# Eight PSUM banks in one pool: retention and feed-forward share them, masks and outputs work on one bank of both units

One NeuronCore of a Trainium2 chip. The metric is device time of the core in microseconds, lower is better; the time before is 290.71 us.

## The reference

Retention (attention without softmax, with a decay mask) feeds a squared-relu feed-forward. Cut to what matters:

```python
batch, n_heads, seq, head_dim = (8, 8, 576, 64)          # q, k, v, float32
gamma = 1.0 - 2.0 ** (-5.0 - np.arange(H))
Dmat = np.where(rel >= 0, gamma[:, None, None] ** rel[None], 0.0)
x = ((q @ k.T / 8) * Dmat) @ v                            # per batch and head
x = x.transpose(0, 2, 1, 3).reshape(4608, 512)
g = np.maximum(x @ w_in, 0.0) ** 2                        # 512 -> 2048
out = g @ w_out                                           # 2048 -> 512, float32
```

## The kernel before

The work is cut into 36 units of 128 tokens, two to a group, 18 groups. For each group TensorE (PE) does

- retention in 64x64 matmuls: scores `psc`, state sums `psS`, outputs `psO`. VectorE (DVE) masks the scores into `rT`, and multiplies the outputs by the decays into `xT`, the input of the feed-forward;
- feed-forward, first half: eight banks `ph` (two row blocks each), relu on ScalarE (ACT) into `rl`, the square on ACT or DVE into `gT`;
- feed-forward, second half, from the third group on as seven Strassen products `po` of eight matmuls, some on sums `gS` that DVE makes. The products live in three banks of the group, called a, b and c.

A Python list scheduler fixes each engine's order at build time. It knows banks only as counters.

```python
    ps_ff = ctx.enter_context(tc.tile_pool(name="ps_ff", bufs=4, space=bass.MemoryType.PSUM))
    ps_ret = ctx.enter_context(tc.tile_pool(name="ps_ret", bufs=1, space=bass.MemoryType.PSUM))
    sched = Schedule(dict(ff=4, prS=1, prO=1, g=3, ...))      # counters: four banks, a score pair, an output pair
    # ... cut ...
    def after_scores(g, t, key):
        for s, u in enumerate(units_of(g)):                   # one instruction a unit, half of both banks
            def fm(s=s, u=u):
                r = tile_of["rT", u] = work.tile([P, 2, NP, 64], FP16, name="rT", tag="rT")
                tile_of["masking", g] = nc.vector.tensor_tensor(
                    out=r, in0=tile_of["psc", g][:, :, cols(s)].rearrange("p a (n i) -> p a n i", i=64),
                    in1=mask.rearrange("p (o r i) -> p o r i", o=1, r=1).to_broadcast([P, 2, NP, 64]), op=ALU.mult)
            m = add("DVE", key + s, 0.7, fm, deps=[t] + ..., acq=("rT",))
        sched.free("prS", [m])
    # ... cut: add_ret, a group not joined with the next ...
            def fa():
                emit_scores(g)
                emit_sums(g, "prO")
            t = add("PE", base + 3, ..., fa, ..., acq=("prS", "prO") if nf else ("prS",))
            after_scores(g, t, base + 5)
    # ... cut: a Strassen product takes its bank from the feed-forward's four ...
                        tile_of["pb", g, bank] = ps_ff.tile([P, HM], FP32, name="po", tag="ff")
```

## Time and profile before

| | before |
|---|---|
| time, median of 3 | 290.71 us (290.68 to 290.76) |
| span of the profiled run, granted clock | 289.1 us, 1.00 |
| busy share PE, DVE, ACT | 98%, 63%, 65% |
| first ph starts / last matmul ends | 17.7 us / 284.8 us |

PE sets the time, and busy share alone does not say how tightly. So the measure used throughout is start to start: from the first matmul of one stretch of feed-forward or of one retention block to the first of the next one, in the timeline.

### The profile page before, as it was taken

What the parts mean: (1) busy time and instruction counts of PE and PEld (TensorE: products, weight loads), DVE (VectorE), ACT (ScalarE), POOL (GpSimd) and SP (SyncE); (2) the same over time, 40 slices, a digit from 0 to 9 for tenths busy, and PEclk for the clock granted to TensorE, in tenths of its full rate; (3) what the DMA queues carried; (4) which work ended last, traced back from release to release, by engine and by line L of the source; (5) the groups of instructions that cost most, each with busy time, mean ns of one, the idle gap of its engine ahead of it and who ended that gap; (6) DMA issues with size and microseconds to landing.
All of it is one profiled execution on the core that took longest, in us unless ns stands there. A gap on an engine that the chain in (4) does not pass through costs nothing.

```text
span 289.1 us, 9988 instructions
## 1 busy us (share of the span) xinstructions
PE 282.1 (98%) x4322; PEld 234.3 (81%) x4322; DVE 182.4 (63%) x381; ACT 188.2 (65%) x361; POOL 84.1 (29%) x121
## 2 busy tenths in 40 slices
PE   8999999999999999999999999999999999999994
PEld 3568755788888888888888888888888888888883
DVE  3772368769585657736686857575777775455622
ACT  5459964685757676767756767676767676747830
POOL 5660035443333243342506061505250500000000
PEclk9999999999999999999999999999999999999999
DMA  7999999999999689999788799899995920201004
GB/s 202 274 208 206 249 291 267 219 203 202 221 188 198 153 201 199 217 219 219 154 199 168 172 194 205 163 196 206 225 182 151 181 76 2 75 2 73 2 8 139
DMA packets 139436, 49.94 MB, mean 173 GB/s; under 512 B 118144, under 2 KB 135040, under 8 KB 139392
## 3 DMA queue, kind: packets, MB, share of 16 engines
q1 hardware_dynamic: 134848, 44.84, 75.3%
q0 software_dynamic: 4224, 4.19, 8.8%
q8 instruction: 34, 0.56, 0.8%
q10 hardware_dynamic: 320, 0.26, 0.4%
q14 instruction: 10, 0.08, 0.1%
HBM read 36.70 MB, written 9.44 MB: 160 GB/s over the span
## 4 chain that ended last, share of the span: by engine, by line
PE 91%; DMA 3%; issue 2%; POOL 2%; DVE 0%; POOLq 0%; DVEq 0%
PE ph L859 44%; PE po L951 34%; PE po L899 5%; PE psO L345 4%; DMA w_in<-in_moe_w_in_dram 3%; PE psc L345 2%; PE psS L345 2%; PE psT L423 1%; POOL mask L215 0%; POOL vx L404 0%; POOL w_in L319 0%; DVE o L974 0%; POOL mask L207 0%; DVE p L1003 0%; POOL mask L211 0%
## 5 line engine op out<-in xcount | busy, mean ns | idle before, releaser
L859 PE MATMUL ph<-xT,w_in 128*128 128x256 f16 x1152 | 139.9, 273 | 0.1
L859 PEld LDWEIGHTS <-w_in 128*128 128x128 f16 x1152 | 110.9, 98 | 14.8 <-DMA w_in<-in_moe_w_in_dram 0.3
L867 ACT ACTIVATE rl<-ph 128x512 f16<-128x512 f32 x144 | 84.5, 588 | 52.5 <-PE ph L859 50.9
L877 ACT ACTIVATE gT<-rl 128x512 f16<-128x512 f16 x118 | 74.4, 631 | 3.4
L951 PEld LDWEIGHTS <-gS 128*128 128x128 f16 x512 | 49.8, 98 | 5.9
L951 PE MATMUL po<-wT,gS 128*128 128x256 f16 x384 | 52.1, 273 | 0.0
L928 DVE TENSOR_TENSOR gS<-gT,gS 128x512 f16<-128x512 f16 x64 | 32.8, 517 | 14.2 <-ACT gT L877 13.5
L951 PEld LDWEIGHTS <-gT 128*128 128x128 f16 x384 | 37.1, 98 | 4.5
L928 DVE TENSOR_TENSOR gS<-gT 128x512 f16<-128x512 f16 x64 | 30.9, 485 | 12.6 <-ACT gT L877 12.5
L359 POOL CAST kq<-k 128x512 f16<-128x512 f32 x28 | 18.6, 663 | 61.4 <-DMA k<-in_k_dram 60.2
L951 PE MATMUL po<-w_out,gT 128*128 128x256 f16 x256 | 34.7, 273 | 0.0
L371 POOL TENSOR_TENSOR v<-v,vdec_full 128x512 f16<-128x512 f32 x24 | 25.4, 1057 | 21.9 <-DMA v<-in_v_dram 20.9
L359 POOL CAST kq<-q 128x512 f16<-128x512 f32 x28 | 18.5, 660 | 30.8 <-DMA q<-in_q_dram 30.6
L964 ACT COPY u<-po 128x256 f32<-128x256 f32 x32 | 11.8, 369 | 19.1 <-PE po L951 18.9
L974 DVE TENSOR_TENSOR o<-po,u 128x256 f32<-128x256 f32 x31 | 13.0, 420 | 16.3 <-PE po L951 10.0
L736 DVE TENSOR_TENSOR xT<-psO,gam_full 128x512 f16<-128x512 f32 x28 | 18.1, 684 | 6.3 <-PE psO L345 6.2
L682 DVE TENSOR_TENSOR rT<-psc,mask 128x512 f16<-128x512 f32 x28 | 18.3, 683 | 4.6 <-PE psc L345 4.5
L879 DVE TENSOR_TENSOR gT<-rl 128x512 f16<-128x512 f16 x26 | 12.8, 492 | 12.6 <-ACT rl L867 11.9
L974 DVE TENSOR_TENSOR o<-po,p 128x256 f32<-128x256 f32 x17 | 7.2, 423 | 17.8 <-ACT u L964 8.8
L951 PE MATMUL po<-wT,gT 128*128 128x256 f16 x128 | 16.8, 273 | 0.0
L951 PE MATMUL po<-w_out,gS 128*128 128x256 f16 x128 | 16.8, 273 | 0.0
L899 PE MATMUL po<-w_out,gT 128*128 128x512 f16 x64 | 15.7, 380 | 0.0
(78 smaller groups left out, 224.0 us busy)
## 6 DMA issues: line engine op xcount, KB each, us to landing
out_dram<-o SPq DMA_DIRECT2D x32, 256.0 KB, 3.7
k<-in_k_dram SPq DMA_DIRECT2D x24, 256.0 KB, 4.8
q<-in_q_dram SPq DMA_DIRECT2D x24, 256.0 KB, 5.1
v<-in_v_dram SPq DMA_DIRECT2D x24, 256.0 KB, 4.9
pair<-in_k_dram SPq DMA_DIRECT2D x4, 512.0 KB, 7.0
pair<-in_q_dram SPq DMA_DIRECT2D x4, 512.0 KB, 7.2
pair<-in_v_dram SPq DMA_DIRECT2D x4, 512.0 KB, 7.0
w_in<-in_moe_w_in_dram POOLq DMA_DIRECT2D x4, 512.0 KB, 8.9
```

What stands on the lines that cost most here:

```text
L345: t = nc.tensor.matmul(out_, lhsT=lhsT, rhs=rhs, start=start, stop=True, skip_group_check=True, tile_position=(64 * row, 64 * col))
L359: op(out=out_.rearrange("p (n b a d) -> p n b a d", n=2, b=2, a=2), in_=in_.rearrange("p (n a b) d -> p n b a d", n=2, a=2))
L371: nc.gpsimd.tensor_tensor(out=t, in0=tile_of["v32", u], in1=vdec[kind].rearrange("p (h o) -> p h o", o=1).to_broadcast([P, H, D]), op=ALU. ...
L682: tile_of["masking", g] = nc.vector.tensor_tensor(out=r, in0=tile_of["psc", g][:, :, cols(s)].rearrange("p a (n i) -> p a n i", i=64), in1 ...
L736: nc.vector.tensor_tensor(out=tile_of["x", g][:, :, s * P:(s + 1) * P].rearrange("p n (c i) -> p c n i", c=2), in0=tile_of["psO", g][:, :, ...
L859: nc.tensor.matmul(tile_of["ph", g, fb][:, j, :], lhsT=w_in16[:, m, fi * P:(fi + 1) * P], rhs=tile_of["x", g][:, m, :], start=(m == 0), st ...
L867: nc.scalar.activation(out=t, in_=tile_of["ph", g, fb], func=ACTF.Relu)
L877: nc.scalar.activation(out=t, in_=rl, func=ACTF.Square)
L899: nc.tensor.matmul(tile_of["po", u], lhsT=tile_of["g", g][:, fi, s * P:(s + 1) * P], rhs=w_out16[:, fi, :], start=(fi == 0), stop=(fi == N ...
L928: nc.vector.tensor_tensor(out=Sx(k, h), in0=in0(h), in1=in1(h), op=op)
L951: nc.tensor.matmul(tile_of["pb", g, bank], lhsT=left(i), rhs=right[:, i, :], start=(start and i == 0), stop=(i == HF - 1), skip_group_chec ...
L974: nc.vector.tensor_tensor(out=o_tile(u)[:, half * HM:(half + 1) * HM], in0=bank(x), in1=tile_of[name, g], op=ALU.add)
```

## The change

The intent: no bank sits idle in a fixed pair; a bank of scores comes free after one mask, not two; feed-forward may use up to eight. The diff, cut to its core:

```diff
-    ps_ff = ctx.enter_context(tc.tile_pool(name="ps_ff", bufs=4, space=bass.MemoryType.PSUM))
-    ps_ret = ctx.enter_context(tc.tile_pool(name="ps_ret", bufs=1, space=bass.MemoryType.PSUM))
+    ps_ff = ctx.enter_context(tc.tile_pool(name="ps_ff", bufs=8, space=bass.MemoryType.PSUM))
-    sched = Schedule(dict(ff=4, prS=1, prO=1, ...
+    sched = Schedule(dict(ff=8, prS=1, prO=1, ...
+    def banks(name):
+        return [ps_ff.tile([P, 512], FP32, name=name, tag="ff") for i in range(2)]
     # after_scores: one instruction a bank, both units
-        for s, u in enumerate(units_of(g)):
-            def fm(s=s, u=u):
+        for a in range(2):
+            def fm(a=a):
-                    out=r, in0=tile_of["psc", g][:, :, cols(s)].rearrange("p a (n i) -> p a n i", i=64),
+                    out=tile_of["rT", g][:, :, a],
+                    in0=tile_of["psc", g][a].rearrange("p (s n i) -> p s n i", s=2, i=64),
+            sched.free("ff", [m])
     # after_outs: likewise xT, one instruction a bank
-                    in0=tile_of["psO", g][:, :, cols(at)].rearrange("p c (n i) -> p c n i", i=64),
+                    in0=tile_of["psO", g][c].rearrange("p (s n i) -> p s n i", s=n, i=64),
     # retention blocks take banks from the common counter
-                    acq=("prS", "prO") if nf else ("prS",))
+                    acq=("prS", "ff", "ff") + (("prO", "ff", "ff") if nf else ()))
-                     acq=("prO", "prS"))
+                     acq=("prO", "prS", "ff", "ff", "ff", "ff"))
     # the first sum quad waits for the mask by an explicit dependency, where reuse of the pair imposed it
+                first_waits.append(tile_of["masking", g + 1])
     # ... cut: the same in the other retention blocks; an unused option (SHARED) removed ...
```

More of the change, by code (lines that the diff above doesn't have):

```diff
@@ L234 @@
     PAIRED = 8
-    SHARED = ()
     FIRST = ["k0", "q0", "v0", "k2", "q2", "v2", "w0", "w1", "w2", "w3", "w4", "w5", "w6", "w7", "k4", "q4", "v4", "k6", "q6", "v6"]
-    sched = Schedule(dict(ff=4, prS=1, prO=1, g=3, ld=5, wst=4, kq=7, v16=7, rT=4, x=3, rl=3, o=4, p1=2, u2=2, u4=2,
+    sched = Schedule(dict(ff=8, prS=1, prO=1, g=3, ld=5, wst=4, kq=7, v16=7, rT=2, x=3, rl=3, o=4, p1=2, u2=2, u4=2,
                           R=5, Rm=2, kqT=6))
@@ L463, in fs @@
             def fs(e=e, tag=tag):
-                ps = rT["ps", e] = ps_ret.tile([P, 2, 512], FP32, name="psc", tag=tag)
+                ps = rT["ps", e] = banks("psc")
                 rT[e] = cast.tile([P, 2, NP, P], FP16, name="rx", tag="kq16")
@@ L467, in fs @@
                     for a, s in ((0, 0), (1, 1), (0, 1), (1, 0)):
-                        quad(ps[half(s), a, hp * P:(hp + 1) * P], kqT(s)[half(a), hp, half(e)], kqT(s)[half(a), NP + hp, :],
+                        quad(ps[a][half(s), hp * P:(hp + 1) * P], kqT(s)[half(a), hp, half(e)], kqT(s)[half(a), NP + hp, :],
                              a, s)
-            t = add("PE", base + 3 + e, 0.4, fs, deps=T["kqT", u] + T["kqT", u + 1], acq=(tag, "kq"))
+            t = add("PE", base + 3 + e, 0.4, fs, deps=T["kqT", u] + T["kqT", u + 1], acq=(tag, "kq", "ff", "ff"))
             ms = []
@@ L474, in fm @@
                     nc.vector.tensor_tensor(
-                        out=rT[e][:, a], in0=rT["ps", e][:, a].rearrange("p (n i) -> p n i", i=P),
+                        out=rT[e][:, a], in0=rT["ps", e][a].rearrange("p (n i) -> p n i", i=P),
                         in1=mask2[:, e].rearrange("p (o e) i -> p o (e i)", o=1).to_broadcast([P, NP, P]), op=ALU.mult)
-                def fc(e=e):
-                    nc.scalar.copy(out=rT[e][:, 1], in_=rT["ps", e][:, 1].rearrange("p (n i) -> p n i", i=P))
-                def fp(e=e):
-                    nc.gpsimd.tensor_tensor(
-                        out=rT[e][:, 1], in0=rT[e][:, 1],
-                        in1=mask2[:, e].rearrange("p (o e) i -> p o (e i)", o=1).to_broadcast([P, NP, P]), op=ALU.mult)
-                if a and g in SHARED:
-                    c = add("ACT", -60 + e, 0.66, fc, deps=[t])
-                    reads = ms + [c]
-                    ms.append(add("POOL", -60 + e, 0.75, fp, deps=[c]))
-                else:
-                    ms.append(add("DVE", base + 5 + e, 0.66, fm, deps=[t] + ms))
-                    reads = ms
-            sched.free(tag, reads)
+                ms.append(add("DVE", base + 5 + e, 0.66, fm, deps=[t] + ms))
+                sched.free("ff", ms[-1:])
+            sched.free(tag, ms)
             masked += ms
         def fk():
-            ps = rT["sum"] = [ps_ff.tile([P, 512], FP32, name="psS", tag="ff") for s in range(2)]
+            ps = rT["sum"] = banks("psS")
             for hp in range(NP):
@@ L541, in put2 @@
             col = h % 2
-            quad(tile_of["psO", g][half(col), s, 128 * (h // 2):128 * (h // 2) + 128], lhsT, rhs, row, col,
+            quad(tile_of["psO", g][s][half(col), 128 * (h // 2):128 * (h // 2) + 128], lhsT, rhs, row, col,
                  start=(g, s, col) not in begun)
@@ L546, in fo1 @@
         def fo1():
-            tile_of["psO", g] = ps_ret.tile([P, 2, 512], FP32, name="psO", tag="prO")
+            tile_of["psO", g] = banks("psO")
             for m in range(NP):
@@ L559, in fo2 @@
             inter(1)
-        t = add("PE", base + 23.9, 0.6, fo1, deps=masked + T["kvx", u], acq=("prO",))
+        t = add("PE", base + 23.9, 0.6, fo1, deps=masked + T["kvx", u], acq=("prO", "ff", "ff"))
         t = add("PE", base + 24, 0.75, fo2, deps=[t, T["R0", g]] + ([T["R", g - 1]] if carry else []))
@@ L574, in fx @@
                     out=tile_of["x", g][:, :, s * P:(s + 1) * P].rearrange("p n (i e) -> p n e i", e=2),
-                    in0=tile_of["psO", g][:, s].rearrange("p (n e i) -> p n e i", n=NP, e=2),
+                    in0=tile_of["psO", g][s].rearrange("p (n e i) -> p n e i", n=NP, e=2),
                     in1=gam_f.rearrange("p n (i e) -> p n e i", e=2), op=ALU.mult)
             T["x", u + s] = add("DVE", base + 25 + s, 0.7, fx, deps=[t] + ([T["x", u]] if s else []), acq=() if s else ("x",))
+            sched.free("ff", [T["x", u + s]])
         sched.free("prO", [T["x", u + 1]])
@@ L602, in emit_scores, with emit_sums @@
     def emit_scores(g):
-        tile_of["psc", g] = ps_ret.tile([P, 2, 512], FP32, name="psc", tag="prS")
+        tile_of["psc", g] = banks("psc")
         for s, u in enumerate(units_of(g)):
             kT = tile_of["kqT", u]
-            ps = tile_of["psc", g][:, :, cols(s)].rearrange("p a (n i) -> p a n i", i=64)
+            ps = [x[:, cols(s)].rearrange("p (n i) -> p n i", i=64) for x in tile_of["psc", g]]
             for hp in range(NP):
                 for a, c in ((0, 0), (1, 1), (0, 1), (1, 0)):
-                    quad(ps[half(c), a, hp, :], kT[half(a), hp, half(c)], kT[half(a), NP + hp, half(c)], a, c)
-    def emit_sums(g, tag):
+                    quad(ps[a][half(c), hp, :], kT[half(a), hp, half(c)], kT[half(a), NP + hp, half(c)], a, c)
+    def emit_sums(g):
         if not full_of(g):
             return
-        tile_of["psS", g] = ps_ret.tile([P, 2, 512], FP32, name="psS", tag=tag)
+        tile_of["psS", g] = banks("psS")
         for s, u in enumerate(units_of(g)):
@@ L619, in emit_sums @@
                 continue
-            ps = tile_of["psS", g][:, :, cols(s)].rearrange("p c (n i) -> p c n i", i=64)
+            ps = [x[:, cols(s)].rearrange("p (n i) -> p n i", i=64) for x in tile_of["psS", g]]
             for hp in range(NP):
@@ L623, in emit_sums @@
                     h = 4 * (hp // 2) + 2 * a + hp % 2
-                    quad(ps[half(a), c, hp, :], tile_of["kq", u][half(c), 0, half(2 * hp + a)],
+                    quad(ps[c][half(a), hp, :], tile_of["kq", u][half(c), 0, half(2 * hp + a)],
                          tile_of["v16", u][half(c), h, :], c, a)
@@ L633, in put @@
         s = units_of(g).index(u)
-        quad(tile_of["psO", g][half(col), c, 256 * s + 64 * (h // 2):256 * s + 64 * (h // 2) + 64], lhsT, rhs, row, col,
+        quad(tile_of["psO", g][c][half(col), 256 * s + 64 * (h // 2):256 * s + 64 * (h // 2) + 64], lhsT, rhs, row, col,
              start=(g, c, col) not in begun)
@@ L648, in emit_out1 @@
     def emit_out1(g):
-        tile_of["psO", g] = ps_ret.tile([P, 2, 512], FP32, name="psO", tag="prO")
+        tile_of["psO", g] = banks("psO")
         for u in units_of(g):
@@ L653, in emit_out2 @@
     def emit_out2(g):
-        for u in units_of(g):
+        for s, u in enumerate(units_of(g)):
             for m in range(NP):
@@ L658, in emit_out2 @@
                     put(g, u, c, h, tile_of["v16", u][half(c), h, :],
-                        tile_of["rT", u][half(c), m % 2, 2 * (m // 2) + b, :], c)
+                        tile_of["rT", g][half(c), s, m % 2, 2 * (m // 2) + b, :], c)
             inter(g, u, 0)
@@ L678, in after_scores @@
     def after_scores(g, t, key):
-        for s, u in enumerate(units_of(g)):
-            def fm(s=s, u=u):
-                r = tile_of["rT", u] = work.tile([P, 2, NP, 64], FP16, name="rT", tag="rT")
+        for a in range(2):
+            def fm(a=a):
+                if a == 0:
+                    tile_of["rT", g] = work.tile([P, 2, 2, NP, 64], FP16, name="rT", tag="rT", bufs=2)
                 tile_of["masking", g] = nc.vector.tensor_tensor(
-                    out=r, in0=tile_of["psc", g][:, :, cols(s)].rearrange("p a (n i) -> p a n i", i=64),
+                    out=tile_of["rT", g][:, :, a],
+                    in0=tile_of["psc", g][a].rearrange("p (s n i) -> p s n i", s=2, i=64),
                     in1=mask.rearrange("p (o r i) -> p o r i", o=1, r=1).to_broadcast([P, 2, NP, 64]), op=ALU.mult)
-            m = add("DVE", key + s, 0.7, fm, deps=[t] + (T["masked", g][-1:] if s else []), acq=("rT",))
+            m = add("DVE", key + a, 0.7, fm, deps=[t] + (T["masked", g][-1:] if a else []), acq=() if a else ("rT",))
+            sched.free("ff", [m])
             T.setdefault(("masked", g), []).append(m)
@@ L696, in fr0 @@
             r = tile_of["Rm", g] = st_pool.tile([P, 2, NP * D], FP16, name="Rm", tag="Rm", bufs=2)
-            x = tile_of["psS", g][:, 0]
+            x = tile_of["psS", g][0]
             if c0:
@@ L704, in fr1 @@
             r = tile_of["tmp", g] = work.tile([P, 2, NP * D], FP32, name="stmp", tag="stmp", bufs=1)
-            nc.vector.tensor_tensor(out=flat(r), in0=tile_of["psS", g][:, 1], in1=flat(tile_of["Rm", g]), op=ALU.add)
+            nc.vector.tensor_tensor(out=flat(r), in0=tile_of["psS", g][1], in1=flat(tile_of["Rm", g]), op=ALU.add)
         def fr2():
@@ L715, in after_sums @@
         T["Rm", g], T["R", g], T["Rread", g], T["Rmread", g] = r0, r2, [], r1
+        sched.free("ff", [r0])
+        sched.free("ff", [r1])
         sched.free(res, [r1])
@@ L723, in after_outs @@
             sched.free("v16", [t2])
-            sched.free("rT", [t2])
             for name, rg, at in states(u).values():
@@ L729, in after_outs, with fx @@
                     sched.free("Rm", [t2, T["Rmread", rg]])
-        for u in us:
-            s, at = groups[g].index(u), us.index(u)
-            def fx(s=s, at=at, u=u):
-                if ("x", g) not in tile_of:
+        sched.free("rT", [t2])
+        for c in range(2):
+            def fx(c=c):
+                if c == 0:
                     tile_of["x", g] = x_pool.tile([P, NP, n * P], FP16, name="xT", tag="xT")
                 nc.vector.tensor_tensor(
-                    out=tile_of["x", g][:, :, s * P:(s + 1) * P].rearrange("p n (c i) -> p c n i", c=2),
-                    in0=tile_of["psO", g][:, :, cols(at)].rearrange("p c (n i) -> p c n i", i=64),
-                    in1=gam[units[u][0]], op=ALU.mult)
-            T["x", u] = add("DVE", key + 0.1 * at, 0.7, fx, deps=[t2] + ([T["x", us[at - 1]]] if at else []),
-                            acq=() if at else ("x",))
-        sched.free("prO", [T["x", us[-1]]])
+                    out=tile_of["x", g].rearrange("p n (s c i) -> p c s n i", s=n, c=2)[:, c],
+                    in0=tile_of["psO", g][c].rearrange("p (s n i) -> p s n i", s=n, i=64),
+                    in1=gam[units[us[0]][0]][:, c].rearrange("p (s n) i -> p s n i", s=1).to_broadcast([P, n, NP, 64]), op=ALU.mult)
+            x = add("DVE", key + 0.1 * c, 0.7, fx, deps=[t2] + ([x] if c else []), acq=() if c else ("x",))
+            sched.free("ff", [x])
+        for u in us:
+            T["x", u] = x
+        sched.free("prO", [x])
     def add_casts(g):
@@ L762, in fa @@
                 emit_scores(g)
-                emit_sums(g, "prO")
+                emit_sums(g)
             t = add("PE", base + 3, 0.2 + 16 * QUAD * (n + nf), fa, deps=scores_deps(g) + sums_deps(g),
-                    acq=("prS", "prO") if nf else ("prS",))
+                    acq=("prS", "ff", "ff") + (("prO", "ff", "ff") if nf else ()))
             for u in units_of(g):
@@ L777, in f2 @@
             def f2():
-                emit_sums(g + 1, "prS")
-                if not full_of(g + 1):
-                    first_waits.append(tile_of["masking", g + 1])
+                first_waits.append(tile_of["masking", g + 1])
+                emit_sums(g + 1)
                 emit_out2(g)
             t1 = add("PE", base + 10, 0.2 + QUAD * (8 * n + 16 * k), f1, deps=out1_deps(g) + scores_deps(g + 1),
-                     acq=("prO", "prS"))
+                     acq=("prO", "prS", "ff", "ff", "ff", "ff"))
             after_scores(g + 1, t1, base + 11)
             t2 = add("PE", base + 30, 0.2 + QUAD * (24 * n + 16 * len(full_of(g + 1))), f2,
-                     deps=[t1] + T["masked", g] + T["masked", g + 1] + sums_deps(g + 1), acq=("prS",) if full_of(g + 1) else ())
+                     deps=[t1] + T["masked", g] + T["masked", g + 1] + sums_deps(g + 1), acq=("prS", "ff", "ff") if full_of(g + 1) else ())
             for u in units_of(g + 1):
@@ L797, in add_ret @@
             t = add("PE", base + 24, 0.45 + 32 * QUAD * n, fb, deps=T["masked", g] + out1_deps(g),
-                    acq=("prO",))
+                    acq=("prO", "ff", "ff"))
             after_outs(g, t, t, base + 27)
```

## The prediction

> **What bounds the kernel now.** I read the page's busy table first, then the row of slices, then the chain that ended last in order of time, then the waits.
>
> ```profile
> PE 282.1 (98%) x4322; PEld 234.3 (81%) x4322; DVE 182.4 (63%) x381; ACT 188.2 (65%) x361; POOL 84.1 (29%) x121
> ...
> PE   8999999999999999999999999999999999999994
> ```
>
> TensorE (PE) is busy in every slice; VectorE (DVE) and ScalarE (ACT) have a third of the span free. That alone doesn't prove saturation, so I checked with starts. One steady group of the chain, where each piece's length is its start to the next one's start:
>
> ```profile
> 203.49 4.47 PE ph L859 x40
> 207.96 1.75 PE po L951 x16
> 209.71 1.31 PE ph L859 x12
> 211.01 0.44 PE po L951 x4
> 211.45 0.44 PE ph L859 x4
> 211.89 1.31 PE po L951 x12
> 213.20 0.44 PE ph L859 x4
> 213.64 0.87 PE po L951 x8
> 214.51 0.25 PE psO L345 x16
> 214.76 0.26 PE psc L345 x32
> 215.02 0.54 PE ph L859 x4
> 215.56 1.75 PE po L951 x16
> 217.31 0.38 PE psS L345 x32
> 217.68 0.40 PE psO L345 x48
> ```
>
> Every feed-forward matmul costs 0.109 us (1.75 / 16), whatever stands before it. The only excess is 0.10 us on the first piece after the 64x64 retention matmuls (0.54 for x4 at 215.02, against 0.44 at 211.45). So a group is 64 ph + 56 po = 120 x 0.1093 = 13.1 us, plus retention 0.25 + 0.26 + 0.38 + 0.40 = 1.3 us, plus two exits of 0.10 us: 14.6 us, and the next group starts at 218.08, 14.59 later. There is no hole in it for a bank to fill.
>
> For the whole run: 1152 ph and 896 Strassen po at 0.1093 are 223.8 us, the 64 po of the first two groups at 0.2155 (a chain piece of 4 takes 0.86) 13.8 us, together 237.6. From the first ph at 17.74 (timeline) to the end of PE at 284.8 (windows: 11.81 us busy after 273.00) are 267.1 us. Adding start to start the pieces that are retention or transposes gives 25.8 us, so 3.7 are left; the 34 exits from retention at 0.10 to 0.11 explain 3.5 and the wait for w_in's last part just before 19.72 about 0.3 (the rest is rounding). Real PE stalls inside are therefore a few tenths of a microsecond at most, some of them inside retention blocks (80 quads took 0.90 us at 160.45 against 0.77 at 217.31).
>
> The waits agree: no row has ph or po waiting for ACT or DVE to give a bank back. It is ACT that waits for PE:
>
> ```profile
> ACT rl L867 <- PE ph L859: 50.9, 48, 2.5
> ...
> PEld L345 <- issue: 9.9, 42, 0.5
> ```
>
> Outside that stretch: 17.7 us ahead (loads, casts, w_in's transfer) and 4.3 us behind (the last add and the stores).
>
> **What the Trainium skill says.** "Perfetto Trace Analysis", Identifying the Most-Contended Engine: matmul busy share is a poor measure of how near PE is to its limit. The trace agrees that it has to be checked: the groups' mean for one ph is 273 ns while its share of time is 109 ns; hence the start-to-start count. The same page, Optimization Strategy: the same gap repeating on an engine that should be saturated can mean too few buffers in SBUF or PSUM. Here the repeating gap is only the 0.10 us exit. "TensorEngine Tiling (Array Packing)", Key Properties: changing the tiling mode drains TensorE; that is what I take the 0.10 us for, and no number of banks changes it. "VectorE: DVE Perf Modes", Why PSUM operands drop a tier: an fp32 operand in PSUM keeps an instruction at one element a cycle. The trace agrees by comparison: 128x512 from PSUM takes 683 ns (rT, xT), an all-f16 tensor_tensor of that size from SBUF about 420 to 520 (gS).
>
> **The change part by part.**
> Pools: four ff banks and two fixed pairs (scores, outputs) become eight ff banks. The counters prS and prO stay, so retention still holds at most two pairs, and feed-forward still has at least four banks; at times up to eight. Saved: only PE waits for a bank, of which I find none to a few tenths in all. Estimate: -0.2 us.
>
> Masks (28 instructions) and outputs xT (28): before, one instruction per unit over half of both banks; now one per bank over both units. Both are 128x512 from fp32 PSUM, in the same number:
>
> ```profile
> L682 DVE TENSOR_TENSOR rT<-psc,mask 128x512 f16<-128x512 f32 x28 | 18.3, 683 | 4.6 <-PE psc L345 4.5
> L736 DVE TENSOR_TENSOR xT<-psO,gam_full 128x512 f16<-128x512 f32 x28 | 18.1, 684 | 6.3 <-PE psO L345 6.2
> ```
>
> So DVE work changes by about nothing: 36.4 us before, 36 to 37 after. The first bank is free one instruction (0.68 us) sooner. This helps only somebody waiting for a bank. Feed-forward of a group needs all of xT, thus both instructions, as before. 0 us.
>
> Order of PE: the kernel orders its instructions by a list scheduler that counts banks. With four, PE writes five ph banks (x40), then must turn to po. Per ph bank PE takes 8 x 0.109 = 0.87 us, and ACT, where it does relu and square, 0.59 + 0.63 with overlap, a step of some 1.15 us (starts 219.10, 220.26, 221.41 in the timeline). With eight banks PE can write all eight ph banks of the group in one run (x64, about 7.1 us) and later run ahead into the next group. PE's amount of work is the same, in another order: 0 us by itself, as long as two retention blocks a group remain; each one merged or split is worth about 0.1 us.
>
> Waits: the retention block f1 now takes four banks that relu, copies or adds have just read, where before it took banks long free. Each first write of a bank may need a wait on ACT or DVE. I reckon 2 to 4 new waits a group, mostly met, at some hundredths of a microsecond each inside a block of fast quads: 14 groups x 0.03 to 0.1 = 0.4 to 1.4 us against, estimated with no row to take it from; but two fixed waits (for prS, prO) go, and ph needs fewer waits with a longer rotation. Net estimate +0.1 us. The explicit wait of the first sum quad on the mask replaces the one that reuse of the score pair imposed: 0.
>
> Sum: -0.2 + 0 + 0 + 0.1 = -0.1; I say 290.5 us.
>
> **Rivals.**
> (1) **Banks were the limit after all**, and longer runs of ph smooth things. For it: PE turns from ph to po after five banks, which is what four banks would enforce. Against: it never idles at the turn. Most it could make is the few tenths of stalls plus part of the 3.5 us of exits if blocks merge: 289 us. Not over 2%.
> (2) **Sharing turns into stalls.** f1 needs four banks at once; the scheduler doesn't reserve, so running ahead with ph can leave fewer than four for a long time; retention comes late, xT comes late, and PE stalls before ph; or the ACT lags the scheduler's assumed times and a retention block sits waiting for a relu. For it: ACT is slower than PE in a ph run (1.15 against 0.87), so long runs build a backlog of about two banks. Against: xT of a group is ready about 13 us before its first ph (219.5 against 232.67), so a late block has nearly a whole group of slack, and ACT has 4.5 us free of each 14.6. At 0.1 to 0.2 us a group this gives 292 to 294; over 2% would need 0.3 us in every one of 18 groups.
> (3) **The ends.** Another order could delay the first ph (it waits for w_in's transfer, untouched) or leave the last products waiting for sums with nothing to fill. PE has no hole after 260 now, and FF1 of the last group can only come earlier with more banks. +0 to +1 us.
>
> **Range and chances.** PE's floor with the same amount of work is about 288.5 to 289 on the timed scale, so 2% faster (under 284.9) would need work to vanish: chance 0.02. The upper side is open through rival 2: 290.5 with a range of 289.0 to 293.0; over 296.5 with chance 0.05. Within 2%: 0.93.
>
> **What would show it.** Right: PE still 280 to 284 us busy; rT and xT still x28 at about 683 ns; ph runs longer than x40 in the chain with po after them; feed-forward pieces at 0.109 each and about 34 exits of 0.10; ACT still waiting for PE. Rival 1 shows as fewer exits or shorter retention blocks. Rival 2 shows as rows of PE or PEld waiting for ACT rl, ACT u or DVE o, retention blocks longer than 0.51 and 0.77 us, or tenths below 9 in PE's row. I am wrong if PE's stretch from the first ph to its end leaves 267.1 by more than 2.5 us, or if either end (17.7, 4.3) moves by more than 1 us.

## More of the kernel before

One stretch will matter, between the two retention blocks of the fifth group (counted from one; `g == 4` in the code). It runs from 62.78 to 69.43 us, 6.65 us. In the timeline of the kernel before (start, length, engine, line, operation, tiles, shapes) its ends and its middle read (`...` marks lines left out):

```profile
62.78 1.05 PE L859 MATMUL ph<-xT,w_in 128*128 128x256 f16 x8
...
64.97 1.04 PE L951 MATMUL po<-w_out,gT 128*128 128x256 f16 x8
...
65.23 0.68 DVE L682 TENSOR_TENSOR rT<-psc,mask 128x512 f16<-128x512 f32 x1
...
69.43 0.31 PE L345 MATMUL psO<-kqT,Rm 64*64 64x64 f16 x8
```

The product po (bank b) runs at once, and the mask of the scores, which had been ready since 62.8, runs beside it. DVE is over two us late with that mask. Nobody minds, because the score pair's banks are retention's own.

## The result, and the profile after

| | before, same rounds | after |
|---|---|---|
| time, median of 4 | 290.69 us (290.56 to 290.76) | 291.75 us (291.47 to 291.94) |
| ratio | | 1.0036, 95% interval 1.0019 to 1.0053: same at 2% |
| span of the profiled run, granted clock | 289.1 us, 1.00 | 289.7 us, 0.996 |
| last matmul ends | 284.8 us | 285.4 us |

The clock of 0.996 costs nothing: the windows of the kernel after show 1.00 in every stretch until 286 us, and a lower one only after PE had ended.

The change is inside 2%, but it is about 1 us slower, and the interval excludes 1. From the page of the kernel after, the busy table, the slices and the start of the chain that ended last:

```profile
PE 281.1 (97%) x4322; PEld 233.3 (81%) x4322; DVE 181.2 (63%) x381; ACT 188.7 (65%) x361; POOL 85.8 (30%) x121
...
PE   7899999998999999999999999999999999999994
...
PE 75%; DVE 1%; issue 0%; DVEq 0%
```

The first two slices, each a tenth lower than before, end at 14.5 us, ahead of the first ph. After them one slice that was 9 is now 8 (the ninth after the first, from 65 to 72 us), and the chain accounts for only 75% on PE, where it was 91%. A chain is followed back from the end to what released each step; here it goes back only to about 65 us and stops at a mask on DVE. Both point to one place. The waits of the kernel after (who waited for whom: us in total, times, longest):

```profile
PEld L346 <- issue: 11.1, 45, 0.5
...
PE po L945 <- DVE rT L673: 0.7, 1, 0.7
```

The second row is new. It happened once. The timeline there:

```profile
62.75 1.05 PE L853 MATMUL ph<-xT,w_in 128*128 128x256 f16 x8
...
63.91 1.26 DVE L922 TENSOR_TENSOR gS<-gT,gS 128x512 f16<-128x512 f16 x1
...
64.51 0.60 PE L945 MATMUL po<-wT,gS 128*128 128x256 f16 x4
...
65.09 0.68 DVE L673 TENSOR_TENSOR rT<-psc,mask 128x512 f16<-128x512 f32 x1
...
65.83 1.03 PE L945 MATMUL po<-w_out,gT 128*128 128x256 f16 x8 [0.71 <-DVE rT L673]
...
70.28 0.31 PE L346 MATMUL psO<-kqT,Rm 64*64 64x64 f16 x8
```

PE stops when its four po end and goes on at 65.83, just after the mask ends at 65.77. The mask is even a little earlier than before (65.09 against 65.23). What is new is that PE waits for it. The stretch takes 7.53 us, start to start, where it took 6.65.

The built program says why: it names the physical bank of every tile. Those around the fifth group's scores, in the order of their first use, with the last reader of each bank's tile before:

```
psc_1331 bank 1   after ph_1226   (read by relu on ACT)
psc_1332 bank 4   after ph_1238   (read by relu on ACT)
psS_1365 bank 2   after ph_1255   (read by relu on ACT)
psS_1366 bank 3   after ph_1266   (read by relu on ACT)
ph_1404  bank 7   after ph_1276   (read by relu on ACT)
ph_1426  bank 0   after ph_1290   (read by relu on ACT)
po_1441  bank 1   after psc_1331  (read by the mask rT on DVE)     <- the product that waits
```

The list scheduler released po_1441 because its counter said that some bank was free. In its plan the mask that holds bank 1 starts after that product, so the bank that it counted was not this one: bank 7, whose relu was done at 64.4 on the chip, would have served. The tile layer handed out the next bank in turn instead.

The rest of the profile is as it was. The groups of the kernel after (count; busy, mean ns):

```profile
L729 DVE TENSOR_TENSOR xT<-psO,gam_full 128x512 f16<-128x512 f32 x28 | 18.1, 685 | 6.5 <-PE psO L346 6.4
...
L673 DVE TENSOR_TENSOR rT<-psc,mask 128x512 f16<-128x512 f32 x28 | 18.3, 683 | 3.4 <-PE psc L346 3.4
```

And the steady group in the chain of the kernel after:

```profile
217.90 0.38 PE psS L346 x32
218.28 0.40 PE psO L346 x48
218.67 4.47 PE ph L853 x40
223.15 1.75 PE po L945 x16
```

Same blocks, same run of x40, same x16 after it. The order of PE's 8644 matmuls and weight loads in the built programs differs from before in only 276 lines of a line-by-line comparison.

In this pair of profiles the account closes (in that of the changed kernel's second profile, below, it needs one more wait): +0.88 us in the fifth group's stretch, then -0.10, -0.12 and -0.06 in three later retention blocks that had been longer before (0.77 to 0.67, 0.90 to 0.78, 0.83 to 0.77), and 0.6 us remain at PE's end.

### The profile page after: what moved, and what is told of

Same layout as the page of the kernel before. It is cut to its first block, busy times and chain, and to the rows that moved or that the text cites. A ratio compares the mean times of both kernels' runs of the same rounds, so it can differ in the third digit from the quotient of the medians.

```text
span 289.7 us, 9992 instructions
## 1 busy us (share of the span) xinstructions
PE 281.1 (97%) x4322; PEld 233.3 (81%) x4322; DVE 181.2 (63%) x381; ACT 188.7 (65%) x361; POOL 85.8 (30%) x121
## 4 chain that ended last, share of the span: by engine, by line
PE 75%; DVE 1%; issue 0%; DVEq 0%
PE ph L853 36%; PE po L945 33%; PE psO L346 3%; PE psS L346 1%; PE psc L346 1%; DVE o L968 0%; DVE rT L673 0%; DVE p L997 0%; DVEq L968 0%
## 5 line engine op out<-in xcount | busy, mean ns | idle before, releaser
L922 DVE TENSOR_TENSOR gS<-gT,gS 128x512 f16<-128x512 f16 x64 | 32.5, 513 | 15.1 <-ACT gT L871 14.5
L372 POOL TENSOR_TENSOR v<-v,vdec_full 128x512 f16<-128x512 f32 x24 | 26.6, 1107 | 20.2 <-DMA v<-in_v_dram 16.9
L873 DVE TENSOR_TENSOR gT<-rl 128x512 f16<-128x512 f16 x26 | 13.4, 517 | 12.4 <-ACT rl L861 11.9
```

The costliest lines, as they stand in the source:

```text
L372: nc.gpsimd.tensor_tensor(out=t, in0=tile_of["v32", u], in1=vdec[kind].rearrange("p (h o) -> p h o", o=1).to_broadcast([P, H, D]), op=ALU. ...
L922: nc.vector.tensor_tensor(out=Sx(k, h), in0=in0(h), in1=in1(h), op=op)
```

## The experiments

**Theory A**: the loss is that one wait, made by sharing: a feed-forward product was given a bank of the score pair, which a late mask still held. **Theory B**: the new forms of masks and outputs, or single banks with more waits, cost it. **Theory C** came later: with shared banks somebody always waits for that mask.

The stretch is the one of the fifth group, start to start in the profile of each run; the ratio is to the kernel before in the same rounds.

| run | stretch us | median us | before us | ratio (95%) |
|---|---|---|---|---|
| before | 6.65 | 290.69 | | |
| after | 7.53 | 291.75 | 290.69 | 1.0036 (1.0019 to 1.0053) |
| after_again | 7.41 | 291.79 | 290.89 | 1.0030 (1.0018 to 1.0043) |
| split | 6.66 | 290.85 | 290.89 | 0.9998 (0.9986 to 1.0011) |
| dose_after | 8.15 | 292.92 | 290.89 | 1.0072 (1.0058 to 1.0085) |
| dose_before | 6.94 | 291.33 | 290.89 | 1.0016 (1.0004 to 1.0029) |
| own_b | 7.18 | 291.41 | 290.66 | 1.0031 (1.0017 to 1.0045) |
| early_mask | 6.65 | 290.75 | 290.66 | 1.0009 (0.9997 to 1.0021) |

### after_again: the changed kernel once more

> The changed kernel unaltered, as a base for the others of this call and because its first profile explains only 0.6 us of the 1.06 us. Theory A (one wait near 65 us: a po bank that the rotation took from the score pair, held until the mask has read it): 291.6 to 291.9 us, and the profile shows that wait again, 0.7 to 1.1 us long, one time. Theory B (per-bank masks and outputs, or finer banks with more waits in the retention blocks, cost it): the same time, but without that wait, with retention blocks above 0.51 and 0.78 us.

291.79 us, with the wait again: 0.59 us, a little below the 0.7 to 1.1 us expected, and the stretch is 0.76 us longer than before. No retention block before 140 us is longer by more than 0.06 us. The loss and the wait repeat. But this profile has a second place, which the first one lacks:

```profile
160.53 1.27 DVE L673 TENSOR_TENSOR rT<-psc,mask 128x512 f16<-128x512 f32 x2
...
161.90 0.45 PE L346 MATMUL psS<-v,kq 64*64 64x64 f16 x32 [0.23 <-issue]
```

The state sums start 0.1 us after the second mask ends (161.80), and in the built program they wait for it; the profile itself names no releaser. The block then takes 0.92 us, against 0.78 in the first profile of the same kernel. In the kernel before the sums depend on the mask too, but there it was done at 159.6. PE ends 0.97 us later than before here, 0.6 in the first profile: the wait in the fifth group is most of the loss, and not all of it in every execution.

### split: the new forms, the old division of banks

```diff
-    ps_ff = ...(name="ps_ff", bufs=8, ...)
+    ps_ff = ...(name="ps_ff", bufs=4, ...)
+    ps_ret = ...(name="ps_ret", bufs=4, ...)      # single banks, tag "ret"
-    sched = Schedule(dict(ff=8, prS=1, prO=1, ...
+    sched = Schedule(dict(ff=4, ret=4, prS=1, prO=1, ...
     # retention takes and frees "ret" where the change has "ff"
```

> The changed kernel with its masks, outputs and single banks, but four banks for feed-forward and four for retention in two pools. Its PE order is that of the kernel before. Theory A: no wait of po on a mask near 65 us; within 0.3 us of the kernel before (290.5 to 291.0). Theory B: stays at 291.5 to 291.9, as the new forms of masks and outputs are all still there.

290.85 against 290.89: equal. In the timeline of split the product starts at once and the mask, just as late, runs beside it:

```profile
64.89 1.04 PE L946 MATMUL po<-w_out,gT 128*128 128x256 f16 x8
64.92 0.68 DVE L674 TENSOR_TENSOR rT<-psc,mask 128x512 f16<-128x512 f32 x1
```

Masks and outputs by bank are all in this kernel and cost nothing, so that part of theory B falls. Two things went back together with the pools, and split alone does not separate them from sharing: the order of PE, which is that of the kernel before to the instruction, and most of the waits (33 of the score and output matmuls carry one, 20 before, 82 after). The runs that follow do: early_mask has all 82 waits, and an order of its own.

### dose_after and dose_before: the same mask twice

```diff
-                tile_of["masking", g] = nc.vector.tensor_tensor(
+                for twice in range(2 if g == 4 and a == 0 else 1):      # s == 0 in the kernel before
+                  tile_of["masking", g] = nc.vector.tensor_tensor(
```

> The changed kernel with the first mask of the fifth group done twice (0.68 us more of VectorE once). Theory A: the wait near 65 us grows by 0.6 to 0.7 us, to about 1.5 us, and the time by 0.4 to 0.7 us over the changed kernel. Theory B: no change of time, below 0.15 us, as VectorE has a third of its time free.

> The kernel before with the same double mask, as control. Both theories: within 0.15 us of the kernel before, since PE does not touch the score pair's banks until the next group. If it is 0.5 us or more slower, the dose itself is on the path and says nothing on sharing.

The timeline of dose_after, then of dose_before:

```profile
65.16 1.41 DVE L674 TENSOR_TENSOR rT<-psc,mask 128x512 f16<-128x512 f32 x2
...
66.63 0.61 PE L946 MATMUL po<-w_out,gT 128*128 128x256 f16 x4 [1.32 <-DVE rT L674]
```

```profile
65.11 1.04 PE L952 MATMUL po<-w_out,gT 128*128 128x256 f16 x8
65.20 1.41 DVE L683 TENSOR_TENSOR rT<-psc,mask 128x512 f16<-128x512 f32 x2
```

With shared banks PE's wait grows from 0.71 us in the first profile (0.59 in after_again) to 1.32 us, by about the added 0.68; without, the product does not notice. So PE is tied to this mask in the one kernel and not in the other. In time both expectations missed: dose_after gained 1.13 us over after_again, more than 0.7, and the control 0.44 us, where I had said at most 0.15, and 0.5 for a control that would say nothing. The control's stretch grew by 0.29 us: behind the doubled mask the add of another product came later (67.12 against 66.43 us), and a ph that reuses that product's bank seems to have waited; the profile names no releaser, so this is read from the starts and from the bank list. The difference of the two, 1.13 - 0.44 = 0.69 us, is about the size of one mask, but by the spread of the five runs each term is uncertain by some 0.3 us: it is the timelines that carry the argument, and this sum only agrees with them.

### own_b: a bank of its own for the product that waited

```diff
-    ps_ff = ...(name="ps_ff", bufs=8, ...)
+    ps_ff = ...(name="ps_ff", bufs=7, ...)
+    ps_b = ...(name="ps_b", bufs=1, ...)           # for the product of bank b alone, counter pb=1
```

> The changed kernel, but seven shared banks and one of its own for the po product that waited near 65 us, so that this product can never be given a bank of the score pair; retention and feed-forward still share the rest. Theory A (the wait is a matter of which bank that one product is given, not of sharing as such): no wait of PE on a mask above 0.3 us, and 290.7 to 291.1 us. Rival C (any sharing makes some feed-forward matmul wait as long, for the next one in line takes the score pair's bank): a wait of 0.5 us or more by a ph instead, 291.4 us or more.

291.41 us. The product no longer waits, but the next in line does:

```profile
65.17 0.68 DVE L674 TENSOR_TENSOR rT<-psc,mask 128x512 f16<-128x512 f32 x1
...
65.90 0.60 PE L854 MATMUL ph<-xT,w_in 128*128 128x256 f16 x4 [0.37 <-DVE rT L674]
```

In the built program this ph has the bank of the first scores, and it waited 0.37 us for the same mask; the stretch is 7.18 us. Neither bound that I had set was met (0.3 us for A, 0.5 us for C), but the direction is C's: taking one product out of the turn moves the wait, it does not remove it. The timed loss, 0.75 us, is larger than the 0.53 us of the stretch; what the rest is stays open.

### early_mask: sharing kept, the mask moved up

```diff
-            m = add("DVE", key + a, 0.7, fm, ...
+            m = add("DVE", key + a - (25 if g == 4 and a == 0 else 0), 0.7, fm, ...
```

> The changed kernel with the first mask of the fifth group set earlier in VectorE's order, ahead of some sums for po. Theory A: the wait of po on the mask near 65 us goes (below 0.2 us), but sums come 0.6 us later and may make po wait there for up to 0.6 us; 290.8 to 291.4 us. If the wait on the mask stays at 0.6 us or more, the lateness of the mask on VectorE is not its cause.

290.75 against 290.66, ratio 1.0009 with an interval that holds 1; slightly better than the 290.8 to 291.4 us expected. The timeline:

```profile
63.23 0.69 DVE L673 TENSOR_TENSOR rT<-psc,mask 128x512 f16<-128x512 f32 x1
...
65.83 1.04 PE L945 MATMUL po<-w_out,gT 128*128 128x256 f16 x8
```

The mask is done at 63.9, two us before the product. The stretch is 6.65 us again, with all eight banks shared; the sums that now come later made nobody wait. The product starts no earlier than in the changed kernel only because a ph went ahead of it and this execution was 0.4 us behind already. (It was the slowest of the five, 291.58 us: its retention block near 48 us takes 1.89 us, against 1.56 to 1.71 in the other kernels so far, and its sums at 161.67 wait 0.25 us as in after_again.)

In the built program the product still gets bank 1, after the same scores: the bank did not change, only the time at which it is free. One thing moved along with the mask: the ph that went ahead fills 0.44 us, which alone would have left some of the 0.71 us wait. What is left of the loss is 0.09 us by the medians and 0.26 by the means, where it was about 0.9 to 1.06, and the interval reaches 0.6. So most of what sharing costs here comes through the lateness of one DVE instruction, and setting that instruction earlier takes most of it back.

### join4, join5, early_join5, early_join6, early_join4: is there a use for shared banks?

In the kernel before, groups from the eighth on are joined: outputs of one group and scores of the next in one block (0.51 us), sums and the rest in another (0.78), against 0.65 and 0.92 for the others. `JOIN = 7` was changed to 4, 5 or 6, in the kernel before (join) and in early_mask (early_join).

> Looking for a kernel faster than both: the kernel before with the joined retention blocks from the fifth group on instead of the eighth. From the profiles a joined group's two blocks take 0.51 + 0.78 us against 0.65 + 0.92, so three groups save 0.8 to 0.9 us: 289.9 to 290.2 us, if the inputs, needed a group earlier, have landed; if they have not, PE waits for transposing transfers and it is 291 us or slower.

> The same from the sixth group on: two groups save 0.5 to 0.6 us, 290.2 to 290.5 us, with less risk of waiting for inputs.

> Looking for a kernel faster than both: shared banks with the early mask (no wait near 65 us) and the joined blocks from the sixth group on. With four feed-forward banks that joining lost, with a 0.7 us wait of a ph on the relu of its bank. If shared banks can help anywhere it is here: such a wait goes, two groups save 0.28 us each, 290.1 to 290.5 us. If running out of banks was not what joining cost, or masks of other groups are waited for instead, 291 to 292 us.

> The same from the seventh group on: one group saves 0.28 us at most, 290.3 to 290.7 us if nothing new is waited for, else 291 us or more.

> The fastest so far once more, unaltered, since five rounds left its ratio at 0.9988 with an interval that reaches 1. Its first profile has no PE wait on ACT or DVE and PE ends 0.7 us earlier than in the kernel before. If that is the kernel's usual state, 290.1 to 290.5 us and a ratio of 0.998 to 0.9995; if the first profile was a lucky one, a ratio of 1 or more.

> The same from the fifth group on, where the kernel with four feed-forward banks lost 3 us. If those were waits for banks as in the sixth group, shared banks take them away: 289.8 to 290.3 us. If they were late sums on VectorE, 292 us or more.

| run | median us | before us | ratio (95%) |
|---|---|---|---|
| join4 | 293.70 | 290.66 | 1.0106 (1.0093 to 1.0119) |
| join5 | 291.97 | 290.66 | 1.0057 (1.0038 to 1.0076) |
| early_join4 | 292.41 | 290.69 | 1.0056 (1.0042 to 1.0070) |
| early_join5 | 290.48 | 290.79 | 0.9988 (0.9974 to 1.0001) |
| early_join5_again | 290.26 | 290.69 | 0.9987 (0.9975 to 1.0000) |
| early_join6 | 291.10 | 290.79 | 1.0019 (1.0005 to 1.0033) |

Joining earlier with four feed-forward banks loses. The chain of join5 shows one reason, the first of two like it:

```profile
95.50 0.61 ACT rl L867
96.11 0.04 issue
96.15 0.60 PE ph L859 x4
```

A ph waits for the relu that still reads its bank. The waits of join4 and join5 have such a row (0.7 us once), those of the kernel before have none: here four banks are too few. The chain of early_join5 at the same place:

```profile
94.63 2.62 PE ph L853 x24
97.25 0.44 PE po L945 x4
```

PE goes on writing ph, and its profile has no PE wait on ACT or DVE from there to the end. Here shared banks help. (early_join5 differs from join5 in the forms and the early mask too; that sharing alone removed the wait was not run.) Both measurements of early_join5 are 0.12 to 0.13% under the kernel before, both intervals end at 1: it may be some 0.4 us faster, and that it is faster is not shown. early_join4 still waits for late sums on DVE and for a copy on ACT (0.5 us each), which more banks do not cure. Why early_join6 is worse than early_join5 I did not find; its profile has one ph waiting 0.3 us for xT.

## Why the prediction was right, and which of its steps were not

The prediction said 290.5 us in 289.0 to 293.0, within 2%; 291.75 us is inside.

- **PE is saturated, more banks cannot help**: right. In the kernel before PE has no wait for a bank, and the change won nothing. The gain of 0.2 us from "PE waits for a bank" did not appear as such; three retention blocks shortened by 0.28 us together in one profile, two of them by 0.17 in the second.
- **Masks and outputs change nothing**: right. 683 and 685 ns for the same 28 and 28 instructions, against 683 and 684.
- **The end and the start keep**: right. The first ph is at 17.74 us in both, and 4.3 us follow the last matmul in both.
- **Order of PE, "all eight ph banks of the group in one run (x64)"**: wrong. The run is x40 as before. I took the turn to po after five banks for the limit of four; the plan shows that these five are the last of the group's eight, the first three having run earlier as fillers, between the po of the group before. The turn comes because the group's ph are done. So the sign "ph runs longer than x40" did not come. This had no effect on the time, but it was the only evidence given for rival 1. The same oversight is in the slack set against rival 2: xT done at 219.5 was said to be ready 13 us before its group's first ph, at 232.67. But that x40 is the rest of the group; its first ph are the fillers at 224.14, so the slack is 4.6 us. It was enough.
- **Waits, "net +0.1 us", as many small waits in every group's retention block**: the term was mis-sized and misplaced. In the built program the score and output matmuls that carry a wait rose from 20 to 82, yet the blocks stayed at 0.51 and 0.77 to 0.78 us: the met waits, whose condition was true when PE came to them, cost nothing that shows. In their place one wait that was not met, 0.59 to 0.71 us long, lengthens one group's stretch by 0.76 to 0.88 us, most of the 0.9 to 1.06 us; a second one, at 161.9 us, shows in one profile of two, and the rest is not assigned. That the loss lies inside the prediction's gross figure for new waits, 0.4 to 1.4 us, and the time inside its range, is luck as far as this mechanism goes: those were many small waits, and the netting down to +0.1 had no number behind it. (The prediction's sum also slips: 290.71 - 0.1 is 290.6, not 290.5.)
- **Rival 2** was the right mechanism with the direction reversed. It spoke of retention waiting for feed-forward's relu; what came was feed-forward waiting for retention's mask. Of its signs, the slice that fell from 9 to 8 came true. The rows to look for were listed as waits on rl, u or o, and the wait was on rT: I had not asked who reads a bank late, only who reads it often.

## What to carry to other kernels

Before making one pool of two, list for each buffer the reader that frees it and how late that reader may run unnoticed: DVE's mask could be over two microseconds late for free as long as its banks were private, and became part of PE's path when they were not. A scheduler that counts free buffers does not decide which one is handed out, so a free count is no promise that the next user won't wait; if sharing is wanted, move the late reader up (one changed priority gave back most of the loss here). Look for a wait for a buffer in the profile before sharing: the kernel before had none, and sharing won nothing there.

## What the Trainium skill lacked or had wrong

- "Perfetto Trace Analysis", Optimization Strategy, says that a repeated gap can be a sign of too few buffers. It has nothing on the other case: here a single gap of 0.7 us came with more buffers in a common pool, and showed as one row in the waits and, past the start, one slice falling from 9 to 8.
- "TensorEngine Tiling (Array Packing)", Key Properties, says that a change of tiling mode drains TensorE, without a size. Here the first four 128x128 matmuls after 64x64 ones take 0.54 us where four take 0.44: 0.10 us each return, 34 times, if the drain is what this is.
- No page that I read says what a met wait on a matmul costs. Here 62 more of them in the score and output blocks left the blocks at 0.51 and 0.78 us.
- No page that I read gives VectorE's time for an operand that lies across two PSUM banks. Here it makes no difference: 683 ns for halves of two banks, 683 ns for one whole bank.
